# The head of a DeltaNet-and-SwiGLU kernel: other unread products, a copy on another engine, a mask in another place

## The chip, the cores and the metric

The kernel runs on one core of one Trainium2 chip. The metric is the device time of one execution in microseconds (us), as the median of several runs. Beside it there is one profiled execution, from which every row below comes.

## The reference

All data are float32. The first stage is a DeltaNet recurrence over 4 batches, 8 heads, 768 positions and head size 48; its output, heads side by side, is the input of a SwiGLU block with a hidden size of 1536:

```python
k_n = k / (np.linalg.norm(k, axis=-1, keepdims=True) + 1e-06)
state = np.zeros((B, H, D, D))
for t in range(S):
    kt, vt, bt = (k_n[:, :, t], v[:, :, t], beta[:, :, t, None])
    y[:, :, t] = np.einsum('bhd,bhde->bhe', q[:, :, t], state)
    v_old = np.einsum('bhde,bhd->bhe', state, kt)
    state = state + bt[:, :, :, None] * np.einsum('bhd,bhe->bhde', kt, vt - v_old)
...
x = y.transpose(0, 2, 1, 3).reshape(B * S, H * D)      # 3072 x 384
g = x @ w_gate
out = ((g * (1 / (1 + np.exp(-g)))) * (x @ w_val)) @ w_out
```

## The kernel before

**Tiling.** The 768 positions are cut into 12 chunks of 64. All 32 pairs of batch and head of a chunk are worked on together: two batches lie in the lower and two in the upper 64 partitions (`b`), and even and odd heads are told apart by `par`. Within a chunk the recurrence becomes a triangular system in the chunk's keys; its solution is what the source calls `uu`. Then come the output `y`, the new state, and the chunk's 256 tokens go through the SwiGLU block. From chunk 2 on the SwiGLU products are arranged in another way, with fewer multiplications (`gate_val_fast`, `output_fast`); the change does not touch them.

**The head.** Until the first SwiGLU product (L1295) the kernel loads keys, queries, values and the first weights and prepares chunks 0 to 3 at once. The steps that the change and the prediction speak of, in program order:

- `unread(5)` (L645): five products of a constant tile `half` with itself, 512 columns each, written to a PSUM bank that is overwritten before anybody reads it. "Unread" means that.
- `turned` transposes keys and queries on TensorE (L505); `gram_steps` multiplies keys with keys, or with `of_q` queries with keys (L521). For queries it is a generator of two parts: the first issues the products, the second the two VectorE multiplications with the mask (L539). `first_q` holds these generators for chunks 0 and 1; chunk 0's products are in banks ffn2 and ffn3, chunk 1's in ffn0 and ffn1.
- `first_substitution` and `first_z` solve for the inverse of the small diagonal blocks on VectorE, and `spread_z` lays this out as `zt` (L736 on ScalarE, L738 on VectorE). `scale_v(0)` scales chunk 0's values (L472).
- the second parts of both `first_q` generators (L539, four instructions of VectorE).
- `small_unread(56)` (L652): 56 products of 32 rows, 32 columns and one moving column each. `warm(1)` (L658): one product with 128 rows, 128 columns and 512 moving columns. Both are unread, and both use the bank p_px.
- `advance(0)`, a generator that the driver steps through. For chunk 0 it issues `n_products` (L747), its two copies to SBUF on ScalarE (L752), and the products of the first solution (L963), whose two halves, by `par`, are copied to `v0` (L972, L973). Three correction steps follow, each of 2 x 16 products (L983, 32 rows of the profile a half), each half followed by an addition on VectorE (L1366), and then the output products (L1061).
- the conversions of the first weights (L272 and L278 on ScalarE, L289, L297 and L309 on VectorE), between the steps of `advance(0)` and behind them.

A float32 product shows as two matmul records and two weight loads in the profile, so 56 products are 112 records.

**What sets the order.** TensorE, ScalarE, VectorE, GpSimd and the SyncE queue each take their instructions in the order in which the source issues them; the order is written out by hand, with semaphores between engines. The SyncE queue loads the weights through `stage`, where GpSimd copies one column (L259) to hold a load back until an earlier one has landed.

**After the head** the chunks' steps are put between the SwiGLU products by `point` and `fill`, so that TensorE always has something to do.

## Time and profile before

| what | value |
|---|---|
| median of 3 runs | 700.45 us (698.83 to 701.66) |
| the profiled execution's span, first to last instruction | 694.7 us |
| TensorE busy in it | 681.7 us, 98% |
| VectorE, ScalarE, GpSimd busy | 411.2, 259.5, 192.3 us |
| first SwiGLU product | 44.61 us after the start |

The profiled execution's own time is known by its span; the timed runs also hold what lies before its first and after its last instruction, and their median is 5.75 us above it. In the timeline a row has its start and its length in us, the engine, the source line, what is written and read, the shape and the number of instructions; in brackets stands how long the engine was idle before it and what ended that. PEld is the loading of a product's weights. In the windows a row has the window, its length, the busy time of TensorE, of its weight loads, of VectorE, ScalarE and GpSimd with the number of instructions, then the granted TensorE clock (1.00 is full speed), the load of the DMA engines and GB/s.

### The profile page before, as it was taken

What the parts mean: (1) busy time and instruction counts of PE and PEld (TensorE: products, weight loads), DVE (VectorE), ACT (ScalarE), POOL (GpSimd) and SP (SyncE); (2) the same over time, 40 slices, a digit from 0 to 9 for tenths busy, and PEclk for the clock granted to TensorE, in tenths of its full rate; (3) what the DMA queues carried; (4) which work ended last, traced back from release to release, by engine and by line L of the source; (5) the groups of instructions that cost most, each with busy time, mean ns of one, the idle gap of its engine ahead of it and who ended that gap; (6) DMA issues with size and microseconds to landing.
All of it is one profiled execution on the core that took longest, in us unless ns stands there. A gap on an engine that the chain in (4) does not pass through costs nothing.

```text
span 694.7 us, 25664 instructions
## 1 busy us (share of the span) xinstructions
PE 681.7 (98%) x11380; PEld 636.3 (92%) x11380; DVE 411.2 (59%) x856; ACT 259.5 (37%) x549; POOL 192.3 (28%) x310
## 2 busy tenths in 40 slices
PE   8899999999999999999999999999999999999997
PEld 4688888757999999999999999999999999999997
DVE  6886789798657755647446456455565345333342
ACT  4774876214442532344233244233143242142230
POOL 5010031106882128820038820328800000000000
PEclk9899999999999999999999999999999999999999
DMA  9578724017550621464423363233363221121210
GB/s 137 151 187 215 215 78 151 1 35 177 128 111 14 116 79 40 105 119 79 93 72 70 74 134 70 56 84 72 67 119 70 56 63 46 55 63 46 69 47 23
DMA packets 143854, 62.31 MB, mean 90 GB/s; under 512 B 122976, under 2 KB 126048, under 8 KB 143744
## 3 DMA queue, kind: packets, MB, share of 16 engines
q1 hardware_dynamic: 141536, 60.19, 37.1%
q8 instruction: 89, 1.46, 0.9%
q10 hardware_dynamic: 2080, 0.39, 0.4%
q0 software_dynamic: 128, 0.10, 0.1%
q14 instruction: 21, 0.17, 0.1%
HBM read 53.58 MB, written 7.08 MB: 87 GB/s over the span
## 4 chain that ended last, share of the span: by engine, by line
PE 96%; ACT 2%; issue 1%; DVE 1%; DVEq 0%; ACTq 0%
PE ffn L1199 43%; PE ffn L1405 20%; PE ffn L1295 9%; PE ffn L1322 4%; PE p_px L963 2%; PE p_px L924 2%; PE p_py L933 2%; PE p_px L1031 1%; PE p_py L521 1%; PE p_py L1019 1%; PE p_px L521 1%; PE p_py L1092 1%; PE ffn L983 1%; PE p_px L645 1%; PE p_px L983 1%
## 5 line engine op out<-in xcount | busy, mean ns | idle before, releaser
L1199 PE MATMUL ffn<-x_ffn,wg_sb 128*128 128x128 f32 x840 | 128.2, 275 | 0.2 <-ACT x_ffn L1098 0.2
L1199 PE MATMUL ffn<-x_ffn,wv_sb 128*128 128x128 f32 x840 | 128.1, 275 | 0.0
L1199 PEld LDWEIGHTS ffn<-x_ffn,wg_sb 128*128 128x128 f32 x840 | 111.1, 192 | 0.3 <-ACT x_ffn L1098 0.3
L1199 PEld LDWEIGHTS ffn<-x_ffn,wv_sb 128*128 128x128 f32 x840 | 110.7, 192 | 0.0
L1234 DVE TENSOR_TENSOR h_f<-sil,ffn 128x256 f32<-128x256 f32 x120 | 49.9, 417 | 78.2 <-ACT sil L1229 76.4
L1229 ACT ACTIVATE sil<-ffn 128x256 f32<-128x256 f32 x120 | 46.1, 384 | 132.5 <-PE ffn L1199 130.8
L1405 PE MATMUL ffn<-wo_sb,h_f 128*128 128x192 f32 x480 | 83.4, 327 | 0.0
L826 POOL TENSOR_TENSOR n_b<-mb,half 128x32 f32<-128x32 f32 x5 | 30.0, 6003 | 183.3 <-DVE mb L563 183.3
L1366 DVE TENSOR_TENSOR ffn<-ffn,p_sb 128x512 f32<-128x512 f32 x58 | 40.5, 698 | 64.1 <-ACT ffn L1255 62.8
L1405 PEld LDWEIGHTS ffn<-wo_sb,h_f 128*128 128x128 f32 x480 | 78.1, 190 | 0.4
L599 POOL TENSOR_TENSOR zb<-zb,tmp 128x31 f32<-128x31 f32 (+15 forms) x124 | 71.4, 576 | 9.7
L593 POOL TENSOR_TENSOR tmp<-zb,mb 128x31 f32<-128x31 f32 (+15 forms) x124 | 67.0, 541 | 16.0 <-DVE mb L580 6.6
L1199 PE MATMUL ffn<-x_t,h_f 128*128 128x128 f32 x480 | 61.0, 280 | 0.2 <-ACT ffn L1212 0.2
L1199 PEld LDWEIGHTS ffn<-x_t,h_f 128*128 128x128 f32 x480 | 56.2, 191 | 1.4 <-ACT ffn L1212 0.4
L1366 DVE TENSOR_TENSOR o_sb<-o_sb,ffn 128x192 f32<-128x192 f32 x49 | 17.2, 352 | 61.9 <-PE ffn L1405 60.7
L1212 ACT COPY ffn<-ffn 128x512 f32<-128x512 f32 x30 | 17.1, 571 | 63.9 <-PE ffn L1199 63.9
L1405 PE MATMUL ffn<-last_k,h_f 128*128 128x192 f32 x200 | 35.9, 327 | 0.0
L1363 DVE TENSOR_TENSOR h_f<-h_f,h_f 128x256 f32<-128x256 f32 x60 | 30.2, 512 | 9.2 <-PE ffn L1405 8.2
L1295 PE MATMUL ffn<-x_ffn,wg_sb 128*128 128x256 f32 x144 | 34.4, 385 | 0.0
L1295 PE MATMUL ffn<-x_ffn,wv_sb 128*128 128x256 f32 x144 | 33.8, 382 | 0.0
L1405 PEld LDWEIGHTS ffn<-last_k,h_f 128*128 128x128 f32 x200 | 32.9, 190 | 0.0
L1295 PEld LDWEIGHTS ffn<-x_ffn,wg_sb 128*128 128x128 f32 x144 | 26.5, 190 | 4.4 <-DVE wg_sb L309 0.8
(304 smaller groups left out, 1100.2 us busy)
## 6 DMA issues: line engine op xcount, KB each, us to landing
h_f<-w_s SPq DMA_DIRECT2D x60, 256.0 KB, 2.8
p_sb<-w_s SPq DMA_DIRECT2D x27, 256.0 KB, 2.6
vin<-in_v_dram SPq DMA_DIRECT2D x48, 96.0 KB, 3.1
out_dram<-o_sb SPq DMA_DIRECT2D x48, 96.0 KB, 2.2
kn<-in_k_dram SPq DMA_DIRECT2D x20, 192.0 KB, 4.5
zt<-in_moe_w_out_dram SPq DMA_DIRECT2D x6, 384.0 KB, 3.6
qpad<-in_q_dram SPq DMA_DIRECT2D x36, 64.0 KB, 3.3
w_s<-h_f SPq DMA_DIRECT2D x7, 256.0 KB, 4.0
```

Source lines behind the costliest of these rows:

```text
L593: engine.tensor_tensor(out=t_v, in0=zb[:, 0 : j + 1, j : j + 1].to_broadcast([128, j + 1, m]), in1=mb[:, j : j + 1, j + 1 : R].to_broadcas ...
L599: engine.tensor_tensor(out=zb[:, 0 : j + 1, j + 1 : R], in0=zb[:, 0 : j + 1, j + 1 : R], in1=t_v, op=ALU.add,)
L826: nc.gpsimd.tensor_tensor(out=n, in0=mb.rearrange("p j i -> p (j i)")[:, 0 : R * R : R + 1], in1=half, op=ALU.pow,)
L1199: nc.tensor.matmul(p[:, u], w(u), moving, start=start and u == 0, stop=True, skip_group_check=True,)
L1212: nc.scalar.copy(p_y, p_x)
L1229: nc.scalar.activation(sil[:, n].rearrange("p (i n) -> p i n", i=2), p[:, 0:2], ACTF.Silu)
L1234: nc.vector.tensor_tensor(out=h_of(c, f, j), in0=sil[:, n].rearrange("p (i n) -> p i n", i=2), in1=p[:, 2:4], op=ALU.mult,)
L1295: nc.tensor.matmul(ps[name][:, i], w_sb[:, t, (f + i) * 128 : (f + i + 1) * 128], xts[c][:, t], start=(t == 0 and i == 0), stop=(t == KT - 1),
L1322: nc.tensor.matmul(p_o, hs[c, f - f % 2][:, f % 2, bp * 128 : (bp + 1) * 128], wo_sb[:, f], start=(f == 0), stop=(f == FT - 1),)
L1363: nc.vector.tensor_tensor(out=out, in0=a, in1=b, op=ALU.subtract)
L1366: nc.vector.tensor_tensor(out=out, in0=a, in1=b, op=ALU.add)
L1405: nc.tensor.matmul(p[x, part], a(f - f % 2)[:, f % 2], b(f), start=not begun and f == 0, stop=f == FH - 1, skip_group_check=True,)
```

## The change

Three things change, all in the head. The 56 small and the one long unread product go, and three products of the kind of the first five take their place. The first half of chunk 0's first solution is copied to `v0` by VectorE instead of ScalarE. And the mask multiplications of chunk 1 (`first_q[1]`) are issued behind the first step of `advance(0)`, so they stand behind that copy in VectorE's queue. No DMA is added, removed or moved.

```diff
-    def small_unread(count):
-
-        p = ps_pair("p_t", "px")[:, 0]
-        for n in range(count):
-            q_ = QUADS[n % 4][0]
-            nc.tensor.matmul(p[q_, 0:1], half[q_], half[q_, 0:1])
-
-    def warm(count):
-
-        p = ps_pair("p_t", "px")[:, 0]
-        for _ in range(count):
-            nc.tensor.matmul(p, ident, kts[0][:, 0:512])
...
         if c == 0:
-            nc.scalar.copy(v0[:, 0], p_u[:, 0])
+            nc.vector.tensor_copy(v0[:, 0], p_u[:, 0])
             nc.scalar.copy(v0[:, 1], p_u[:, 1])
...
         scale_v(0)
-        for steps_of in first_q:
-            next(steps_of)
-        small_unread(56)
-        warm(1)
+        next(first_q[0])
+        unread(3)
         new_nt(0, qpad[1].rearrange("p bp h d -> p (bp h d)"))
         zb_1 = work.tile([128, R, R], FP32, name="zb", bufs=1)
         new_nt(1, zb_1.rearrange("p k i -> p (k i)"))
         step("advance", advance, 0)
+        next(first_q[1])
```

The function that stays and is called once more:

```python
def unread(count):
    p = ps_pair("p_t", "px")[:, 0]
    for _ in range(count):
        nc.tensor.matmul(p[0:R], half, half[:, 0:1].to_broadcast([128, 512]))
```

The changed kernel's lines behind the removed functions stand 13 lower than the lines named here.

## The prediction

> **What bounds the kernel now.** I read the page first, then the chain that ended last, then the head (the first 45 us, where the whole change lies) engine by engine in the timeline, and last the windows of that stretch.

> ```profile
> span 694.7 us, 25664 instructions
> ...
> PE 681.7 (98%) x11380; PEld 636.3 (92%) x11380; DVE 411.2 (59%) x856; ACT 259.5 (37%) x549; POOL 192.3 (28%) x310
> ...
> q8 instruction: 89, 1.46, 0.9%
> ...
> PE 96%; ACT 2%; issue 1%; DVE 1%; DVEq 0%; ACTq 0%
> ```

> TensorE is busy 98% of the span and holds 96% of the chain, so the end moves only by what moves TensorE. No edit touches the loops after the head: the change can be worth only what the head's own waits and clock are worth, a few us of 694.7. The q8 row (packets, MB, share of the DMA engines) matters below: 89 packets against 11380 products plus 11380 weight loads is 256 TensorE instructions a packet, so I take q8 as TensorE's instruction stream.

> TensorE in the timeline, around the edit:

> ```profile
> 23.59 1.11 PE L521 MATMUL p_py<-last_k 64*64 64x64 f32 x64
> 24.53 1.11 PE L521 MATMUL ffn<-qt,kt 64*64 64x64 f32 x64
> 25.57 0.30 PE L652 MATMUL p_px<-half 32*32 32x1 f32 x16
> 27.16 0.97 PE L652 MATMUL p_px<-half 32*32 32x1 f32 x96 [1.29 <-issue]
> 28.06 2.07 PE L658 MATMUL p_px<-kt,ident 128*128 128x512 f32 x2
> 30.07 1.75 PE L747 MATMUL p_py<-zt,a_sb 64*64 64x64 f32 x63
> 31.65 0.21 PE L963 MATMUL p_px<-vin,zt 64*64 64x48 f32 x2
> 31.66 0.22 PE L747 MATMUL p_py<-zt,a_sb 64*64 64x64 f32 x1
> 31.66 1.14 PE L963 MATMUL p_px<-vin,zt 64*64 64x48 f32 x62
> 33.42 1.02 PE L983 MATMUL ffn<-v,qpad 64*64 64x48 f32 x28 [0.63 <-ACT v L972]
> 35.11 1.26 PE L983 MATMUL ffn<-v,qpad 64*64 64x48 f32 x36 [0.67 <-issue]
> 36.18 4.01 PE L983 MATMUL ffn<-uu,qpad 64*64 64x48 f32 x128
> ...
> 44.61 1.73 PE L1295 MATMUL ffn<-x_ffn,wg_sb 128*128 128x256 f32 x6
> ```

> Two idle stretches end in "issue", nothing that the profile shows: 1.29 us among the small products, 0.67 us among the first correction products (L983). Between their ends lie 96 + 2 + 63 + 2 + 1 + 62 + 28 = 254 products with as many loads, 508 instructions, almost twice 256. I read both as waits for the next block of instructions. A block starts 128 products before the gap at its end. Counting back, the first wait's preceding block was entered at product 17 of the 23.59 row, about 23.83, and its successor came at 27.16: 3.33 us. For the second it is product 30 of the 30.07 row, about 30.8, and 35.11: 4.3 us. TensorE idles whenever it runs a block faster than that.

> The clock, with windows cut where it changes:

> ```profile
> 10.95:14.37 3.42, 2.20 (x123) 1.55 (x120) 2.22 (x13) 1.20 (x3) 1.22 (x1) 1.00 1.28 150
> 14.37:17.78 3.41, 3.15 (x54) 2.61 (x42) 2.46 (x6) 2.78 (x9) 1.00 (x4) 0.50 0.97 165
> 24.61:28.02 3.41, 2.12 (x184) 1.97 (x175) 3.07 (x11) 2.54 (x7) 0.27 (x2) 1.00 0.50 159
> 28.02:31.43 3.41, 3.41 (x65) 1.89 (x59) 3.38 (x7) 0.94 (x2) 0.37 (x2) 0.50 0.47 131
> 31.43:34.85 3.42, 2.39 (x117) 2.19 (x110) 1.24 (x3) 2.93 (x6) 0.18 (x1) 1.00 0.59 176
> 34.85:38.26 3.41, 3.15 (x108) 3.14 (x108) 1.66 (x3) 3.41 (x9) 0.37 (x2) 1.00 0.50 151
> ```

> The first figure after the length is TensorE's busy time; the clock is third from the end. A window with 2.20 or 2.12 us busy was followed by one at half clock; one with 2.39 was not. So 28.02 to 31.43 runs at 0.50, and the long product and the L747 products pay for it.

> **Part 1, the unread products.** Removed: 56 small ones (112 passes with 112 loads, 224 instructions) and the long one (4). Added: 3 of the kind that opens the kernel, 6 passes and 6 loads. Their price, from the weight loads of the first five:

> ```profile
> 2.74 0.18 PEld L645 LDWEIGHTS p_px<-half 128*32 128x32 f32 x1 [0.68 <-issue]
> 3.60 0.18 PEld L645 LDWEIGHTS p_px<-half 128*32 128x32 f32 x1 [0.68 <-issue]
> 5.16 0.11 PEld L645 LDWEIGHTS p_px<-half 128*32 128x32 f32 x1 [0.32 <-issue]
> 5.59 0.11 PEld L645 LDWEIGHTS p_px<-half 128*32 128x32 f32 x1 [0.32 <-issue]
> ```

> A pass takes 0.86 us early and 0.43 later. After 24.61 the clock is full: 6 x 0.43 = 2.6 us, from 25.57 to 28.16. The block that came at 27.16 is now needed only 20 instructions past the three products, ten products into L747, so the 1.29 us wait lies under them. The window 24.61 to 28.02 is busy throughout, so I expect full clock from 28.02 on.

> L747 then waits for its operand. The other engines:

> ```profile
> 28.36 1.05 DVE L738 TENSOR_SCALAR zt<-mb,m_rows 128x512 f32<-128x512 f32 x2
> 29.31 0.97 DVE L472 TENSOR_TENSOR vin<-vin,n_t 128x768 f32<-128x768 f32 x1
> 30.18 2.49 DVE L539 TENSOR_TENSOR p_sb<-ffn,mask_q 128x512 f32<-128x512 f32 x4
> 35.54 0.55 DVE L1366 TENSOR_TENSOR uu<-v,ffn 128x384 f32<-128x384 f32 x1 [2.87 <-PE ffn L983]
> 40.24 0.55 DVE L1366 TENSOR_TENSOR uu<-v,ffn 128x384 f32<-128x384 f32 x1 [0.38 <-PE ffn L983]
> 28.36 0.79 ACT L736 ACTIVATE zt<-mb,m_rows 128x256 f32<-128x256 f32 x1 [0.18 <-DVE mb L727]
> 31.92 1.07 ACT L752 COPY qpad<-p_py 128x512 f32<-128x512 f32 x2 [2.77 <-PE p_py L747]
> 32.88 0.50 ACT L972 COPY v<-p_px 128x384 f32<-128x384 f32 x1
> 33.25 0.51 ACT L973 COPY v<-p_px 128x384 f32<-128x384 f32 x1
> 39.01 0.43 ACT L272 ACTIVATE wv_sb<-h_f 128x256 f32<-128x256 f32 x1
> 36.02 0.18 POOL L259 COPY h_f<-h_f 128x1 uint32<-128x1 uint32 x1 [0.45 <-DMA h_f<-in_moe_w_val_dram]
> ```

> VectorE spreads z until 28.36 + 1.05 = 29.41 and ScalarE until 29.15; nothing ahead of that changes. So L747 starts at 29.45 instead of 30.07, behind 1.3 us of idle TensorE. At the rate of L521 (64 in 0.94 us at full clock) it ends at 30.4 instead of 31.7; v is scaled at 30.28, just in time. L963 takes 1.1, to 31.5 instead of 32.80.

> **Part 2, the copy on VectorE.** L972 takes 0.50 on ScalarE; L1366, which reads as many elements of PSUM, takes 0.55 on VectorE. The first correction product waits for this half alone and stood 0.62 after L963's end; I take 0.67, so 32.2. The path loses 0.05. In the built program ScalarE's half waits for VectorE's: about 32.15 to 32.65. It is read after 32 products (128 L983 products in 4.01 us, 0.031 each), at 33.2, so 0.5 us covers that. Behind it on ScalarE stand the spread for chunk 1 and the weight steps, all earlier than before; the last pair of weights that these read had landed by 36.02 and was read at 39.01, 3.0 us of slack.

> **Part 3, chunk 1's mask later.** Half of the 2.49 us, 1.25, moves behind the copy: 32.1 to 33.4 on VectorE. Queued behind it is the first L1366. It issues no DMA. Its readers come with chunk 1's output, after 44.61.

> **The sum.** The next block of instructions is entered ten products into L747, at 29.6, and needed ten products into L983 (54 + 64 + 10 = 128), at 32.5. It comes after 3.33 to 4.3 us: 32.95 to 33.9, middle 33.4. So this wait grows from 0.67 to some 0.9 us. From there 22 products x 0.031 and the 0.31 us that lay between the last product and 35.54 give the first add at 34.4, 1.1 us early; the mask, done at 33.4, is covered by 1.0 us, and by nothing if the block came at once. One block later, 128 x 0.031 = 4.0 us on, the wait is 0 to 0.3. Net at the last add: 1.0 us early (0.5 to 1.6 by the two block times). The conversions behind the adds and L1295 follow by as much.

> Against it stands the clock. The window 28.02 to 31.43 will have 0.14 + (31.43 - 29.45) = 2.1 us busy. The next one has the copy's wait of 0.7 and the block wait of 0.9 together: about 2.15 us (1.7 to 2.6). Both are at the level that was followed by half clock. Its price: L747 took 1.58 / 63 = 25 ns at 0.50, L521 0.94 / 64 = 15 at 1.00, so 1.7 times. A full window of L983 then loses 3.41 - 3.41 / 1.7 = 1.4 us, less 0.1 for the second block wait, which it hides; in 31.43 to 34.85, where L983 fills some 1.7 us, 0.7 are lost.

> **Forecast, one half-clock window in L983's stretch:** 1.0 - 0.7 = 0.3 gained or 1.0 - 1.3 = 0.3 lost; I take 0.1 gained. The profiled execution goes from 694.7 to 694.6, and the median of the three timed runs, 5.75 above that span, from 700.45 to 700.3. Its own range, with 0.5 either way for the block times, is 699.5 to 701.3.

> **Rivals.**
> A, the clock stays full. For it: the window with 2.39 us busy was let through, and how busy counts is unknown; products that fill the array may count for more than small ones, and L747 and L963 fill it better than the small unread ones did. Then the whole 1.0 stays: 699.4, down to 698.3 if no block is late (L983 runs from 32.2, first add at 33.4, 2.1 early). [...]

> B, the slower side: half clock in two windows, 31.43 to 38.26. Place: L983. It decides if the first half-clock window, holding the block wait, is itself too idle to be released; those that were released before had 3.15 and 3.41 us busy, this one would have 2.2 to 2.4. Price: 0.7 + 1.4 - 1.0 = 1.1 lost, 701.5; a third window over the rest of L983 and the output products makes it 702.5.

> C, the change brings TensorE forward by little: both blocks come as late as 4.3 us, so the stop at L983's tenth product takes half of the gain, and a half-clock window comes on top: 0.5 - 1.3 = 0.8 lost, 701.2. For it: the later of the two measured blocks took that long; against it, the other took 3.33, and both would have to be late.

> **How the numbers follow.** Forecast 0.50, A 0.25, B 0.19, C 0.06. Time 700.3. The timed runs spread from 698.83 to 701.66, so the median of a few can lie 1 us off. The range runs from A's with its lower bound to B's: 698.0 to 702.4. The bound of 0.5% is 3.5 us, about what a measurement of this kernel can tell from no change; no case reaches it alone. A without block waits plus a lucky spread gives faster 0.03; B with a third window and an unlucky spread gives slower 0.03; same 0.94.

> **What would show it.** Right: no issue wait before 28; three products from 25.57 to 28.2; PEclk 1.00 in 28.02 to 31.43; L747 from 29.45; an issue wait about ten products into L983; the first L1366 near 34.4; 0.50 in one window after 31.43. Wrong: 0.50 already from 28.02 (32 columns don't hold the clock), no issue wait in L983, the first L1366 behind the mask and not behind TensorE, or L1295 starting over 1.5 us from 44.6.

## The result and the profile after

The changed kernel takes 697.37 us (median of 22 runs, 694.44 to 699.9). The kernel before took 699.3 us beside it on the same chip (22 runs, 696.51 to 705.54). The ratio is 0.9965, 95% interval 0.995 to 0.9979. In a second comparison it was 0.9966 (0.9952 to 0.9981). So 1.9 to 2.5 us are gained, 0.35%, clearly more than nothing and less than the 0.5% that the prediction set as its bound. The predicted 700.3 us and the range from 698.0 miss it: 1.15 us of that because the three runs of before lay high (700.45 against 699.3), the rest, 1.8 us, because the gain was put at 0.1. Ratios are of fast runs: two slow executions among the experiments below, of 861.89 us (28 small products) and 3881.52 us (copy and mask only), are in the medians and not in the ratios.

The page of the changed kernel, the same lines as of before:

```profile
span 695.9 us, 25446 instructions
PE 680.5 (98%) x11272; PEld 634.9 (91%) x11272; DVE 410.3 (59%) x857; ACT 258.7 (37%) x548; POOL 192.3 (28%) x310
...
q8 instruction: 88, 1.44, 0.9%
...
PE 93%; SPq 2%; DMA 2%; ACT 1%; issue 1%; DVE 1%; POOL 0%; DVEq 0%; ACTq 0%
```

Its span is 695.9 us, longer than the 694.7 of the profiled execution before, although the kernel is faster by its runs: two single executions need not stand in the order of the medians. TensorE in the timeline, through the head:

```profile
25.38 2.77 PE L645 MATMUL p_px<-half 128*32 128x512 f32 x6
29.77 1.16 PE L734 MATMUL p_py<-zt,a_sb 64*64 64x64 f32 x64 [1.63 <-ACT zt L723]
30.76 1.10 PE L950 MATMUL p_px<-vin,zt 64*64 64x48 f32 x64
32.70 0.43 PE L970 MATMUL ffn<-v,qpad 64*64 64x48 f32 x8 [0.84 <-DVE v L959]
34.46 2.68 PE L970 MATMUL ffn<-v,qpad 64*64 64x48 f32 x56 [1.33 <-issue]
36.83 4.74 PE L970 MATMUL ffn<-uu,qpad 64*64 64x48 f32 x128
...
46.26 0.92 PE L1282 MATMUL ffn<-x_ffn,wg_sb 128*128 128x256 f32 x3
```

The wait among the small products is gone; TensorE stands ready 1.63 us ahead of z and starts L734 (L747 before) at once. The wait for "issue" is now inside the first correction (L970, before L983). The other engines, and the windows:

```profile
28.19 1.01 DVE L725 TENSOR_SCALAR zt<-mb,m_rows 128x512 f32<-128x512 f32 x2
31.99 0.56 DVE L959 COPY v<-p_px 128x384 f32<-128x384 f32 x1 [0.72 <-PE p_px L950]
32.47 1.28 DVE L539 TENSOR_TENSOR p_sb<-ffn,mask_q 128x512 f32<-128x512 f32 x2
35.47 0.55 DVE L1353 TENSOR_TENSOR uu<-v,ffn 128x384 f32<-128x384 f32 x1 [1.72 <-PE ffn L970]
...
41.61 0.55 DVE L1353 TENSOR_TENSOR uu<-v,ffn 128x384 f32<-128x384 f32 x1 [0.38 <-PE ffn L970]
29.00 0.72 ACT L723 ACTIVATE zt<-mb,m_rows 128x256 f32<-128x256 f32 x1
```

```profile
28.33:31.74 3.41, 1.97 (x128) 1.96 (x128) 2.94 (x5) 2.13 (x5) 0.84 (x2) 1.00 0.52 138
31.74:35.16 3.42, 1.25 (x41) 1.06 (x35) 1.75 (x3) 2.91 (x5) 0.37 (x2) 1.00 0.49 147
35.16:38.57 3.41, 3.41 (x72) 3.41 (x70) 1.11 (x2) 3.41 (x12) 0.32 (x2) 0.50 0.50 159
```

One window at 0.50, in L970, as forecast. The first addition (L1353, before L1366) waits 1.72 us for TensorE and not for the mask. The last one starts at 41.61.

### The profile page after: what moved, and what is told of

It reads as the page before. It is cut to its first block, busy times and chain, and to the rows that moved or that the text cites. A ratio compares the mean times of both kernels' runs of the same rounds, so it can differ in the third digit from the quotient of the medians.

```text
span 695.9 us, 25446 instructions
## 1 busy us (share of the span) xinstructions
PE 680.5 (98%) x11272; PEld 634.9 (91%) x11272; DVE 410.3 (59%) x857; ACT 258.7 (37%) x548; POOL 192.3 (28%) x310
## 3 DMA queue, kind: packets, MB, share of 16 engines
q8 instruction: 88, 1.44, 0.9%
## 4 chain that ended last, share of the span: by engine, by line
PE 93%; SPq 2%; DMA 2%; ACT 1%; issue 1%; DVE 1%; POOL 0%; DVEq 0%; ACTq 0%
PE ffn L1186 43%; PE ffn L1392 20%; PE ffn L1282 9%; PE ffn L1309 4%; PE p_px L950 2%; PE p_px L911 2%; PE p_py L920 2%; PE p_px L1018 1%; PE p_py L1006 1%; PE p_py L521 1%; SPq L140 1%; PE p_px L521 1%; PE ffn L970 1%; DMA h_f<-in_moe_w_gate_dram 1%; PE p_py L1079 1%
## 5 line engine op out<-in xcount | busy, mean ns | idle before, releaser
L1186 PEld LDWEIGHTS ffn<-x_ffn,wg_sb 128*128 128x128 f32 x840 | 111.1, 192 | 0.1
L1186 PEld LDWEIGHTS ffn<-x_ffn,wv_sb 128*128 128x128 f32 x840 | 110.7, 192 | 0.0
L1353 DVE TENSOR_TENSOR ffn<-ffn,p_sb 128x512 f32<-128x512 f32 x58 | 40.5, 699 | 63.7 <-ACT ffn L1242 62.4
L1353 DVE TENSOR_TENSOR o_sb<-o_sb,ffn 128x192 f32<-128x192 f32 x49 | 17.2, 352 | 61.9 <-PE ffn L1392 60.7
L1282 PEld LDWEIGHTS ffn<-x_ffn,wv_sb 128*128 128x128 f32 x144 | 27.0, 190 | 3.7
```

The lines of the kernel that those rows point to most:

```text
L1186: nc.tensor.matmul(p[:, u], w(u), moving, start=start and u == 0, stop=True, skip_group_check=True,)
L1282: nc.tensor.matmul(ps[name][:, i], w_sb[:, t, (f + i) * 128 : (f + i + 1) * 128], xts[c][:, t], start=(t == 0 and i == 0), stop=(t == KT - 1),
L1353: nc.vector.tensor_tensor(out=out, in0=a, in1=b, op=ALU.add)
```

## The experiments

All ratios are to the kernel before in the same comparison; its median there was 698.65 (first four kernels), 699.03 (next four), 698.1 (next four), 698.97, 700.02 and 698.96 us, so only ratios are compared between groups. The expectations name theories by letters. I: the instructions of the 56 small products cost the time. B: the waits for "issue" are for the next block of 256 TensorE instructions, and what counts is where the borders fall. K: the clock alone decides. Z: what matters is how long the unread work keeps L747 waiting behind z. C, F, S and V are explained where they first stand; this C is not the prediction's rival C.

### Which part of the change: four kernels

The kernel before, unchanged, as a second sample and for its trace:

> The kernel before, unchanged, for a second trace and for the spread of its executions. Theory C (clock: the change lowers the number of half-clock windows an execution meets, each worth about 1.4 us): the granted clock of its executions is mostly 0.994 to 0.995 (two windows), where the changed kernel's 22 executions lie from 0.994 to 1.0, and slower executions have the lower clock. Theory F (instruction blocks: the small products cost a block wait of 1.3 us that the change hides): clock as in the changed kernel, and the trace shows the 1.3 us issue wait among the small products again. Theory S (the profiled execution of before was a lucky one): its span now comes out 2 to 3 us over 694.7.

Measured: 699.86 us, ratio 1.0016 (0.9998 to 1.0034), no difference, as it must be. Its profile spans 694.9 us, so theory S is not met as it was put; but its 696.62 us was the lowest of its 12 runs, so this trace too stands at the low end of the spread. The issue wait among the small products is there again, 1.36 us at 27.14, as theory F has it.

The exchange of the unread products alone:

```diff
-        small_unread(56)
-        warm(1)
+        unread(3)
```

> Only the unread products are exchanged; the copy stays on ScalarE and the mask in its place. If the products are the cause (theories C and F alike): ratio to before 0.9965 as for the whole change, 2.4 us faster. If the copy and the mask are (theory V: VectorE's copy starts at once, ScalarE is relieved): about 1.000.

Measured: 697.3 us, 0.9981 (0.996 to 1.0001), which by itself is not clear of no change. The copy and the mask alone:

```diff
-            nc.scalar.copy(v0[:, 0], p_u[:, 0])
+            nc.vector.tensor_copy(v0[:, 0], p_u[:, 0])
...
-        for steps_of in first_q:
-            next(steps_of)
+        next(first_q[0])
...
+        next(first_q[1])
```

> Only the copy moves to VectorE and chunk 1's mask behind it; the 56 small and the long product stay. Theories C and F: 1.000 (699.3 us or within 0.7 us of before). Theory V: 0.9965.

Measured: 699.36 us, 0.9993 (0.9965 to 1.0021). The changed kernel with no unread product there at all (`unread(3)` deleted):

> The changed kernel without the three unread products: TensorE idles from about 25.4 until z is spread at 29.5. Theory C (the unread products are there to hold the clock): a half-clock window follows in the stretch 28 to 35, granted clock 0.994 to 0.995, and 1 to 1.5 us slower than the changed kernel, so about 0.998 to 1.000 of before. Theory F (what counts is that the small products' instructions are gone): as fast as the changed kernel, 0.9965.

Measured: 698.39 us, 1.0002 (0.9983 to 1.0021), with a mean granted clock over its runs of 0.992, against 0.9965 in the changed kernel. What follows: the copy and the mask are worth nothing that can be measured; the gain must come with the products (clear of noise only in later kernels, 0.9971 twice, below); and some unread work is needed. In the profile of this last kernel L734 still starts with z, at 30.05, but after 3.08 us of idle TensorE, and it takes 2.13 us for 61 products instead of 1.16 for 64:

```profile
30.05 2.13 PE L734 MATMUL p_py<-zt,a_sb 64*64 64x64 f32 x61 [3.08 <-ACT zt L723]
```

### How much unread work, and where the border falls: four kernels

The changed kernel with a few small products between the long ones, which moves the next border by 24 instructions, so that it should fall near the end of the first solution's products:

```diff
-        unread(3)
+        unread(1)
+        small_unread(6)
+        unread(2)
```

> The changed kernel with six small products (24 instructions) between the first and the second unread product. The block of TensorE instructions that now begins ten products into L734 then begins among the small ones, and the next one among the last products of L950 instead of eight into L970. Theory B (an issue wait is the fetch of 256 instructions, 3.3 to 4.8 us after the block before was entered): the issue wait of 1.3 us in L970 is gone, at most 0.7 us of waiting lies among the unread products, the window around 32 to 35 us is busier and not followed by half clock: 1.3 to 1.9 us faster than the changed kernel, 0.994 to 0.9955 of before. If issue waits are something else: no change against the changed kernel, 0.9965, and the wait stays in L970.

Measured: 698.54 us, 0.9987 (0.9972 to 1.0003), slower than the changed kernel. The border fell behind 61 of the 64 products, as foretold, but the block took about 5 us to come, more than the 3.3 to 4.8 of the expectation, and was waited for longer than anywhere so far, 1.95 us where at most 0.7 was expected. Nor did the clock hold: 35.38 to 42.21, two windows, ran at 0.50.

```profile
31.82 1.09 PE L957 MATMUL p_px<-vin,zt 64*64 64x48 f32 x61
34.85 0.31 PE L957 MATMUL p_px<-vin,zt 64*64 64x48 f32 x3 [1.95 <-issue]
```

Five unread products instead of three, `unread(5)`:

> The changed kernel with five unread products in place of three: 4.3 us on TensorE, nearly the 4.5 to 5 us of before, but 20 instructions instead of 228. Theory Z (length): 1.2 to 1.7 us slower than the changed kernel, ratio to before 0.998 to 0.999, and in the trace L734 starts at the end of the fifth product, 1 us or more after z is there. Theory I (the 224 instructions of the small products and their block wait): as the changed kernel, 0.9965. Theory C (the clock held): clock and time as the changed kernel or better.

Measured: 696.73 us, 0.9951 (0.9936 to 0.9966). Two instead of three, `unread(2)`:

> The changed kernel with two unread products: 1.7 us. Theory Z: as the changed kernel where z is the later one, up to 0.9 us faster where TensorE is, so 0.9955 to 0.9965. Theory C: one more half-clock window in some executions, clock 0.994 to 0.995, and 0.5 to 1 us slower than the changed kernel, 0.9970 to 0.998. With no unread products at all the clock was 0.992 and the time 698.27 us on average.

Measured: 696.3 us, 0.9948 (0.9932 to 0.9965). The changed kernel itself once more:

> The changed kernel, unchanged, next to the variants below and for a second trace. Theory Z (z is usually laid out before TensorE has finished the unread products, so their whole length counts, and before spent 4.5 to 5 us on them against 2.6 now): L734 starts within 0.1 us of the end of the z spread or of the third product, whichever is later; ratio 0.9965, granted clock 0.996 to 0.997 on average. All theories give the same ratio here.

Measured: 696.94 us, 0.9966 (0.9952 to 0.9981). What follows: theory Z falls. Five products end only when z is done and hold L734 back 0.75 us, and still the time is at least as good.

### The small products by themselves: four kernels

The kernel before without them, `warm(1)` kept (`small_unread(56)` deleted):

> The kernel before without its 56 small products; the one long product stays, and so do the copy and the mask. Theory I (the 224 instructions of the small products cost a block wait of 1.3 to 1.8 us right before L747, wherever the clock stands): at equal granted clock 1 to 2 us faster than before, ratio 0.997 to 0.9985, the clock itself being no better than before (0.992 to 0.995) because one product of 0.9 us holds it less than three. Theory K (only the clock counts, and the small products do nothing for it or against it): no faster than before, 1.000, and no offset at equal clock.

Measured: 695.76 us, 0.9971 (0.9953 to 0.9988). And the changed kernel with them put back:

```diff
         next(first_q[0])
+        small_unread(56)
         unread(3)
```

> The changed kernel with the 56 small products put back in front of the three unread ones. Theory I: the issue wait of 1.3 to 1.8 us is back among the small products, L734 starts 1.5 us or more behind z, and the kernel is 1.2 to 2 us slower than the changed kernel, 0.9985 to 0.9995 of before, though its clock is that of the changed kernel (0.996). Theory K: as the changed kernel, 0.9965.

Measured: 698.69 us, 0.9999 (0.9982 to 1.0015). Taking away the small products alone gives the whole gain; putting them back takes it all. So theory K falls as well: the clock alone does not decide (mean 0.9955 without them, 0.9951 in the runs of before beside it). In the profile of the kernel with them:

```profile
28.21 0.30 PE L652 MATMUL p_px<-half 32*32 32x1 f32 x16
29.87 0.97 PE L652 MATMUL p_px<-half 32*32 32x1 f32 x96 [1.36 <-issue]
30.77 4.43 PE L645 MATMUL p_px<-half 128*32 128x512 f32 x6
35.13 1.16 PE L741 MATMUL p_py<-zt,a_sb 64*64 64x64 f32 x64
```

```profile
27.34:30.75 3.41, 2.05 (x177) 1.90 (x168) 3.23 (x8) 3.10 (x8) 0.39 (x2) 1.00 0.53 163
30.75:34.17 3.42, 3.42 (x14) 0.72 (x6) 1.92 (x3) 0.00 (x0) 0.19 (x2) 0.50 0.54 160
```

The wait of 1.36 us leaves a window with 2.05 us busy; the next one runs at 0.50, the three products take 4.43 us instead of 2.77, and L741 starts 4.5 us behind z. Two repeats stood beside these, the kernel with two unread products and the kernel before:

> The changed kernel with two unread products once more, since only six executions of it were left to compare. If two are better than three: 0.995 of before and 696 us; if they are alike: 0.9965 and 697.

> The kernel before, for a third trace. The two traces so far are of executions at the fast end of its spread (696.4 and 696.6 us of 694.9 to 703.2). Theories I and K alike: in an execution near the median (699 us) the z spread ends 1 us or more before L747 starts, and one more half-clock window or block wait than in those two shows in the first 50 us. Ratio 1.000.

Measured: 695.76 us, 0.9965 (0.9948 to 0.9982), and 698.52 us, 1.0006 (0.9989 to 1.0024). So two unread products are like three. The third trace of before is of an ordinary execution, 698.24 us, and what was expected of it did not come: L747 stands 0.34 us behind z, not 1 us or more. Its lateness was there before the edited lines are reached. Its five opening products took 7.47 us instead of 6.01, and z was laid out at 31.39 instead of 29.41:

```profile
1.03 7.47 PE L645 MATMUL p_px<-half 128*32 128x512 f32 x10 [1.03 <-DVE half L316]
```

In the execution profiled first the same row is:

```profile
1.03 6.01 PE L645 MATMUL p_px<-half 128*32 128x512 f32 x10 [1.03 <-DVE half L316]
```

There the record of the full clock begins at 4.13 us, in the third at 7.09.

### By number or by borders: five kernels

Other numbers of small products in the kernel before, `small_unread(28)`, `small_unread(84)`, and later `small_unread(12)`:

> The kernel before with 28 small products instead of 56. With 56 the loss against none was 2.1 us (ratio 0.9971 without them). Theory of number, each of the 224 instructions costs its share: half the loss goes, 1.05 us, ratio 0.9985. Theory of blocks: the border of the block that is waited for lies 32 instructions into the small products, so it stays and so does its wait; only the 56 records behind it go, 56 x 10 ns = 0.57 us, ratio 0.9992, and an issue wait of 1.2 to 1.7 us is still seen among the small products. Theory that any small product is in the way: no gain, 1.000.

> The kernel before with 84 small products instead of 56. Theory of number: 1.05 us slower, ratio 1.0015. Theory of blocks: a second border now falls among the small products, 256 instructions behind the first, and its block comes 3.1 to 5.5 us after the first one (4.4 typical): in the execution profiled before that is 27.16 + 4.4 = 31.6, then 48 records of the small ones and the long product, 1.5 us, so L747 starts near 33 instead of 30.07 and the kernel is 2.5 to 3 us slower, ratio 1.004, with two issue waits among the small products. Theory that any small product is in the way: 1.000.

> The changed kernel with one unread product instead of three (0.9 us on TensorE in place of 2.8), so z is waited for by TensorE idle for about 3 us. If the clock decides here: the window before L747 is then as empty as without unread products, where the mean clock was 0.992 and the time 1.0 us above the changed kernel's: ratio 0.999 to 1.000. If one product is enough, as two were: 0.995 to 0.997.

Measured: with 28 701.93 us, 1.0029 (1.0007 to 1.0052); with 84 702.89 us, 1.0057 (1.0036 to 1.0078); the changed kernel with one unread product 696.82 us, 0.997 (0.9949 to 0.9991), so one product is enough. The theory of number falls: half of them cost more than all. With 84 the second wait came as theory B said:

```profile
27.05 0.30 PE L652 MATMUL p_px<-half 32*32 32x1 f32 x16
29.26 1.77 PE L652 MATMUL p_px<-half 32*32 32x1 f32 x128 [1.91 <-issue]
32.99 0.50 PE L652 MATMUL p_px<-half 32*32 32x1 f32 x24 [1.96 <-issue]
33.42 2.08 PE L658 MATMUL p_px<-kt,ident 128*128 128x512 f32 x2
35.42 1.99 PE L747 MATMUL p_py<-zt,a_sb 64*64 64x64 f32 x64
```

Between the two waits lie 128 products with 128 loads, 256 instructions. The execution then ran at half clock in five windows in a row, 29.48 to 46.55. The answer for 28 was against theory B as I had worked it out (0.9992), so it was repeated, with 12 beside it:

> The kernel before with 28 small products once more. If the loss is real: 1.001 to 1.005 again, at a mean clock below that of before, and its profile shows the issue wait among the small products, then a second idle stretch ahead of L747, because TensorE is through with its unread work before z, and half clock in a window behind the two. If the loss belonged to that chip or call: 0.997 to 1.000, halfway to the kernel without small products.

> The kernel before with 12 small products, 48 instructions. The border that is waited for lies 32 instructions into them, so its wait is there but only 16 instructions and the long product lie behind it. Theory of the wait as idle time ahead of a half-clock window: as with 28, 1.001 to 1.005. Theory that the work behind the border costs, because it delays L747: 1.1 us of it are left, z hides it, and the ratio is that of no small products, 0.997.

Measured: 28 again 702.44 us, 1.0059 (1.0034 to 1.0085); 12 698.35 us, 0.9975 (0.9954 to 0.9996). The loss with 28 is real. In its profile it is not where I had expected it, in a second idle stretch ahead of L747, but at the borders behind:

```profile
28.14 0.50 PE L652 MATMUL p_px<-half 32*32 32x1 f32 x40 [1.36 <-issue]
29.87 1.19 PE L747 MATMUL p_py<-zt,a_sb 64*64 64x64 f32 x61 [0.17 <-ACT zt L736]
33.41 0.90 PE L963 MATMUL p_px<-vin,zt 64*64 64x48 f32 x43 [1.97 <-issue]
...
57.24 0.32 PE L963 MATMUL p_px<-vin,zt 64*64 64x48 f32 x5 [1.29 <-issue]
...
251.62 0.32 PE L901 MATMUL p_py<-t,z 32*32 32x32 f32 x14 [1.62 <-issue]
...
349.24 0.21 PE L901 MATMUL p_py<-t,z 32*32 32x32 f32 x2 [1.15 <-issue]
```

With 28 small products the head has 112 instructions fewer, and the waits for "issue" behind it stand at other instructions than in the first profile of before, which has them at 53.31, 68.18 and 449.17 us. Here they fall into dense stretches of small products up to 349 us, far behind anything that the edit touches: the part behind the first SwiGLU product takes 654.1 us, 4.0 more than the 650.1 of before. With 12 the second border falls into L963 too (1.36 us of waiting at 33.13), and yet the time is nearly that without small products; so not every such wait ahead of the first SwiGLU product costs its length, and the expectation that the work behind the border decides is met.

The table sums, for each profiled execution, the idle time of TensorE in front of the first instruction of each block (records 449 + 256 k, counting products, loads and the semaphore instructions of TensorE's own queue in the order in which they start), from 20 us on. Each row is one execution, the ratio that of the runs:

```
kernel                      L747 behind   border waits   first     span    ratio
                            z, us         head / rest    SwiGLU    less it
before (profiled first)     0.66          1.96 / 1.67    44.61     650.1
before, again               1.21          2.37 / 2.06    44.46     650.4   1.0016
before, third               0.34          1.77 / 1.92    46.64     649.9   1.0006
copy and mask only          2.56          3.23 / 1.75    49.12     649.9   0.9993
small put back              4.52          3.87 / 1.23    51.34     649.0   0.9999
84 small                    4.50          4.40 / 2.41    53.01     650.8   1.0057
28 small, again             0             3.47 / 5.09    46.65     654.1   1.0059
12 small                    0             3.00 / 2.55    45.90     651.7   0.9975
changed                     0.05          1.44 / 1.96    46.26     649.6   0.9965
changed, again              0.04          0.49 / 2.28    44.84     650.5   0.9966
products only               0             1.47 / 2.55    46.05     650.7   0.9981
no small, warm(1) kept      0             0.38 / 1.85    43.82     650.2   0.9971
unread(5)                   0.75          0.07 / 1.04    43.74     649.0   0.9951
unread(2)                   0             1.85 / 1.19    45.52     649.2   0.9948
unread(2), again            0             1.30 / 1.04    45.56     649.2   0.9965
unread(1)                   0             1.73 / 1.08    44.83     650.0   0.9970
no unread product           0             0.38 / 1.39    47.36     649.6   1.0002
six small between           0.21          2.75 / 0.61    48.99     648.6   0.9987
```

With 56 or more small products the border waits of the head are 1.8 to 4.4 us, in the kernels without any 0.1 to 1.9.

### The copy, and the last candidate

In every profile with the copy on VectorE the first correction product stands 0.81 to 0.84 us behind the first solution's products, without it 0.57 to 0.65. So the last kernel has two unread products, with copy and mask as before:

```diff
-        small_unread(56)
-        warm(1)
+        unread(2)
```

> The kernel before with two unread products in place of the small ones and the long one; the copy on ScalarE and the mask stay as they were. If the copy on VectorE costs what the rows show, 0.2 us, the first correction product stands 0.6 us behind the first solution's products instead of 0.84, and the time is that of the changed kernel with two unread products less 0.2: ratio 0.9945 to 0.9960. If the later mask is worth more than that (it takes 1.25 us of VectorE out of the way of the copy), 0.996 to 0.998.

Measured: 696.91 us, 0.9971 (0.9954 to 0.9988); the first correction product stands 0.65 us behind:

```profile
30.07 1.17 PE L747 MATMUL p_py<-zt,a_sb 64*64 64x64 f32 x64 [1.70 <-DVE zt L738]
31.05 1.11 PE L963 MATMUL p_px<-vin,zt 64*64 64x48 f32 x64
32.81 0.55 PE L983 MATMUL ffn<-v,qpad 64*64 64x48 f32 x10 [0.65 <-ACT v L972]
33.65 1.77 PE L983 MATMUL ffn<-v,qpad 64*64 64x48 f32 x54 [0.29 <-issue]
```

The 0.2 us is in the rows but not in the times: 0.9971 lies in the second range, and its interval reaches into both. The versions with one, two, three or five unread products or the long one alone all lie between 0.9948 and 0.9981, and their intervals overlap; none is shown to beat the change.

## Why the prediction was wrong

**Most of its steps in the head came.** No issue wait stands among the unread products; there are three of them from 25.38, 2.77 us long (forecast 2.6); the clock is full in 28.33 to 31.74; L734 starts at the end of z's spread (29.00 + 0.72 on ScalarE), at 29.77 (forecast 29.45); an issue wait stands behind eight products of L970 (forecast ten), 1.33 us (forecast 0.9); the mask is hidden; one window behind 31.43 is at 0.50.

**Their sum in that execution did not come.** The first addition came at 35.47 instead of 34.4: L970 began 0.5 us later than forecast (32.70 against 32.2), and its wait was 0.4 us longer. Of the 1.1 us that it was to come early, 0.07 was left against 35.54 before. The half-clock window, 35.16 to 38.57, then lay wholly on L970 and took the dearer of the two prices: first to last addition went from 4.70 to 6.14 us, 1.44 lost (forecast 1.3). The first SwiGLU product came at 46.26, 1.65 us behind the 44.61 of before, which is the prediction's own sign of being wrong ("L1295 starting over 1.5 us from 44.6"), on the slower side. In the second profile of the changed kernel it came at 44.84, after an issue wait of 0.49 us.

**The copy's term was too small.** 0.67 us was forecast between the last product of the first solution and the first of the correction, 0.05 lost; the row of L970 shows 0.84, 0.2 lost. It moves the time by nothing that the runs show.

**The step that failed** is the price of the small products, read off one execution and carried over to the median: "The profiled execution goes from 694.7 to 694.6, and the median of the three timed runs, 5.75 above that span, from 700.45 to 700.3." They were charged only with what z did not hide in that execution, 30.07 less 29.45, 0.62 us at L747, and with the change's other terms 0.1 us was left. The runs show about 2 us: 0.9971 when they alone are taken away, 0.9999 when they are put back into the changed kernel.

**The base was no ordinary execution.** Run times are 1.7 us above their spans (697.58 for the span of 695.9), so only 1.7 of the 5.75 us between span and median are time outside the span. The execution profiled before, 694.7, was a run of about 696.4 us, below the lowest of the 22 runs of before beside the change (696.51 to 705.54); of the 164 runs of this kernel beside the experiments 10 took 696.4 us or less. The profiles of the changed kernel are of runs of 697.58 and 697.03 us, the middle of its spread. So the two kernels' profiles set one from the low end beside two from the middle, which is enough for the changed kernel's to look the slower. The change does not only shorten the long runs: beside each other the lowest runs are 694.44 and 696.51 us, the highest 699.9 and 705.54.

**What the small products cost in the head** differs from one execution to the next. L747 started 0.34, 0.66 and 1.21 us behind z in three profiles of the same kernel, 2.56 with the copy and mask changed, 4.5 with more unread work behind them. No execution of before slower than 698.24 us was profiled. The nearest is the kernel with copy and mask changed, in a run of 700.68 us, whose TensorE work up to L747 is that of before. There the border among the small products is waited for, 30.99 to 34.40 is at 0.50, and the long product and L747 lie in that window:

```profile
30.32 1.07 PE L652 MATMUL p_px<-half 32*32 32x1 f32 x96 [1.66 <-issue]
31.32 2.08 PE L658 MATMUL p_px<-kt,ident 128*128 128x512 f32 x2
33.32 1.67 PE L747 MATMUL p_py<-zt,a_sb 64*64 64x64 f32 x63
```

**Where the gain lies stays open.** The border waits of the head fell from 2.03 us (mean of the three profiles of before) to 0.97 (two of the changed kernel), 1.1 us; and the mean granted clock of the runs rose by 0.002 (from 0.994 to 0.995 in different comparisons to 0.9965 and 0.9968). Among the runs of before, 0.001 of clock goes with 0.2 to 0.4 us, so the clock goes with 0.4 to 0.8 of the 2.2 to 2.5 us by which the means differ. But the shorter waits did not bring these five executions forward: from the end of z's spread to the first SwiGLU product they take 15.2, 15.6 and 15.2 us before and 16.5 and 15.4 us in the changed kernel. That the small products cost the time is shown by taking them out and putting them back; by which wait or window they do is argued, and would need profiles of both kernels at like places among their runs.

**The rivals.** A, the clock stays full, had nearly the right size (down to 698.3), but in both profiles of the changed kernel the clock fell where the forecast said (35.16 and 34.68); in the first of them the window ahead of it, 31.74 to 35.16, had 1.25 us busy and two gaps of 0.84 and 1.33 us. The near hit is luck as far as these profiles go. That products which fill the array count for more towards the clock, as A supposed, no run shows by itself. B, half clock in two or more windows there, did not happen in the two profiles of the changed kernel, but in that with 84 small products it did, in five windows. C's late block came too: the one that L970 waited for began 4.6 us after the one before it (29.9 to 34.46), more than the 4.3 that C took. By its runs the kernel gained all the same; by this one execution it did not.

## What to carry to other kernels

One profiled execution is a sample: before summing against it, set its span, plus the few us around it, beside the lowest and the highest run, and compare it only with a profile that stands at a like place among its own runs. Unread work that bridges a wait did better here as few long products than as many short ones: the ratios are 0.9948 to 0.9981 with one to five long ones and 1.0029 to 1.0059 with 28 or 84 small ones, and the profiles with 56 small ones, 224 instructions, have an idle stretch of 1.3 to 1.7 us among them. An edit that changes the number of TensorE instructions is worth following through the whole trace: with 28 small products waits for "issue" of 1.62 and 1.15 us stood at 251.62 and 349.24 us, hundreds of us behind the edit, where the first profile of before has none.

## What was not expected of the hardware

- The idle stretches of TensorE over 0.15 us that "issue" ends, from 20 us on, all end at the same place of a block of 256 instructions, semaphore instructions counted (90 of 90 in 20 traces, to one instruction). There the next block was entered 2.6 to 5.3 us after the one before it (2.9 to 4.3 in the first profile of before, 4.3 to 5.1 in that of the changed kernel); the prediction had put it at 3.33 to 4.3. In two experiments that moved the stretch it fell where it was foretold: behind 61 of 64 products with the six small ones, and 256 instructions behind the first with 84.
- The half-clock stretches in the head are 3.41 us long each in the first profile of either kernel (14.37 to 17.78 and 28.02 to 31.43 before, 35.16 to 38.57 in the changed kernel) and do not start at the same place in each execution. Nor does the full clock: its record begins at 4.13 us in the execution profiled first, at 4.44 in the changed kernel's and at 7.09 in the third of before, and the five opening products took 6.01, 6.16 and 7.47 us. So the two executions of before were 1.98 us apart at the end of z's spread (29.41 and 31.39), before anything that an edit touches. And the wait for "issue" in the first correction lay on both sides of 34.85, where one 3.41 us window of the first profile ends (34.44 to 35.11), but inside the window from 31.74 to 35.16 in the changed kernel's (33.13 to 34.46).
- Busy time alone does not tell in these traces which window is followed by half clock: in the changed kernel one with 1.97 us was not, one with 1.25 was; with 84 small products windows with 3.32 and 3.41 us busy at half clock were followed by half clock again:

```profile
29.48:32.89 3.41, 1.55 (x123) 1.46 (x112) 3.41 (x7) 1.40 (x3) 1.10 (x2) 0.50 0.40 98
32.89:36.31 3.42, 3.32 (x58) 1.80 (x62) 0.55 (x1) 0.00 (x0) 0.37 (x2) 0.50 0.57 159
36.31:39.72 3.41, 2.81 (x110) 2.65 (x102) 0.00 (x0) 1.64 (x4) 0.37 (x2) 0.50 0.53 155
39.72:43.13 3.41, 3.41 (x64) 3.41 (x66) 0.55 (x1) 3.41 (x7) 0.37 (x2) 0.50 0.32 99
43.13:46.55 3.42, 3.42 (x68) 3.42 (x68) 1.11 (x2) 2.88 (x9) 0.48 (x3) 0.50 0.96 230
46.55:49.96 3.41, 3.41 (x124) 3.41 (x124) 2.37 (x6) 0.35 (x1) 0.00 (x0) 1.00 0.88 217
```
